# The weighted sum over V in a fused attention and gated feed-forward kernel: V made the stationary operand in 64x32 array tiles, two head groups at once, with the output turned by VectorE transposes and packed by DMA

## The chip, the cores and the metric

The kernel runs on one core of a Trainium2 chip. The metric is the device time of one execution in microseconds (us), median over several executions. Executions of one kernel agree to about 0.3%.

## The reference

A block of a transformer on a sequence of 2,048 tokens of width 576: a layer norm, then sliding-window attention (32 heads of width 18, window 256) and a gated feed-forward of width 4,608 on the same normalised input, multiplied together and added to the input.

```python
xn = layernorm(x)                                   # [2048, 576]
q, k, v = split(xn @ wqkv)                          # 32 heads, Dh = 18
scores = q @ k.T * 18**-0.5                         # masked: 0 <= i - j < 256
s = (softmax(scores) @ v) @ wo
h = sigmoid(xn @ w_gate) * (xn @ w_up)              # F = 4608
out = x + s * silu(h @ w_down)
```

## The kernel before

The tokens are handled in four chunks of 512. (Two memories are named below: SBUF holds the operands, PSUM the results of matmuls.) In each chunk the kernel projects q, k and v, runs attention for eight groups of four heads, applies `wo`, and runs the feed-forward network. A list scheduler inside the program fixes the order of every engine's instructions before the launch, from a small table of estimated durations. It places gate/up and down matmuls wherever attention leaves TensorE free.

Scores are computed with keys on the partitions, so that after the exponential a tile `expr` holds [64 keys x queries]. For the weighted sum over V (called PV below) the kernel before makes `expr` the stationary operand and streams V (18 columns and a column of ones for the softmax sum), so each matmul has 19 or 38 moving columns. (The stationary operand sits in the array; the columns of the moving one stream past it.) The array is used as two tiles of 64 rows by 128 columns. In all code cuts here `...` stands for what is left out, some arguments are put in words, and comments are added.

```python
def pair(eng, outs, lhs, rhs, start, stop, swap=0):
    for i in range(2):                               # two 64-row tiles of the array
        t = i ^ swap
        res = eng.matmul(outs[i], lhs(ROWS[t], i), rhs(ROWS[t], i), ..., tile_position=(64 * t, 0))

# build_attn(c, hg): one PV group per group of four heads
for qb in range(BPC):                                # 4 blocks of 128 queries
    for t in range(2):
        ...
        for n, ks in enumerate(kss):                 # key blocks that all 128 queries see
            res = pair(eng, [b[:, o:o + VH] for b in outs],
                       lambda r, i: self.expr[r, se, t, qb * P:(qb + 1) * P],     # stationary, 64x128
                       lambda r, i: vpart(r, sub_pos(c, ks) * VSZ + hh), ...)     # moving, 64x19
        ...                                          # and one pair with 2 x 19 columns for the two edge blocks
# VectorE: two sums of two parts each, a reciprocal, two multiplies, per group
sm = op("DVE", ..., tensor_reduce(out[ROWS[i]], src, X, ALU.add))     # i = 0, 1
rc = op("DVE", 250, reciprocal(out[:, :, DH], out[:, :, DH]))
on = op("DVE", ..., tensor_tensor(o_tok[...], src, rr, ALU.mult))     # par = 0, 1
...
# build_wo(c): o_tok is turned by DMA transposes before the wo projection
te = self.flip(self.oT[:, so, :, :], self.o_tok[:, i, :], ...)
```

The softmax here doesn't subtract the row's maximum and nothing guards it: scores larger than these inputs give would overflow.

## Time and profile before

| what | value |
|---|---|
| time, median | 576.02 us (575.97 to 577.16, 3 runs) |
| span of the profiled execution | 575.1 us |
| PV on TensorE, first start to the next work's first start, 32 groups | 30.8 us |

The page's first part has, for each engine, the busy time, its share of the span and the count of instructions (PE is TensorE's matmuls, PEld its weight loads, DVE VectorE, ACT ScalarE, POOL GpSimd):

```profile
PE 568.3 (99%) x9324; PEld 358.6 (62%) x9324; DVE 339.1 (59%) x825; ACT 268.3 (47%) x379; POOL 176.7 (31%) x286
```

The page's fourth part is the chain of waits that ended last, followed back from the last instruction, as shares of the span by engine:

```profile
PE 94%; DVE 2%; DMA 1%; issue 1%; ACT 1%; POOL 1%; DVEq 0%
```

Both say TensorE (PE). They have to be read together: a busy share alone does not say who waits for whom, and the records of matmuls overlap.

The groups of instructions by line and shape (out<-in, shapes, count, busy us, mean ns of one, idle time before):

```profile
L99 PE MATMUL ps<-xnT,wgs 64*128 64x512 bf16 x2256 | 281.2, 376 | 0.0
...
L762 DVE TENSOR_REDUCE pvs<-ps 64x304 f32<-64x608 f32 x64 | 50.4, 787 | 11.9 <-PE ps L99 10.2
...
L99 PE MATMUL ps<-v_aug,expr 64*128 64x19 bf16 x1920 | 34.9, 168 | 0.0
...
L774 DVE TENSOR_TENSOR o_tok<-pvs 128x144 bf16<-128x144 f32 x64 | 16.8, 303 | 0.3
...
L766 DVE RECIPROCAL pvs<-pvs 128x16 f32<-128x16 f32 x32 | 8.0, 249 | 0.0
```

The lines L99 are matmuls, all of one helper; the tiles tell them apart. A 19-column matmul lasts 168 ns in its record, a 512-column one 376 ns: what both have in common is a latency of about 160 ns, which overlaps from one matmul to the next. So mean durations of matmuls must not be added. The three VectorE lines are the path behind PV: two reductions of 787 ns for each group, one reciprocal, two multiplies. For TensorE, what counts is the distance between starts, and the timeline shows it (start, length, engine, line, shapes, count):

```profile
351.67 0.83 PE L99 MATMUL ps<-xnT,wgs 64*128 64x512 bf16 x6
352.32 1.19 PE L99 MATMUL ps<-v_aug,expr 64*128 64x19 bf16 x80
353.33 0.40 PE L99 MATMUL ps<-xnT,wgr 64*128 64x512 bf16 x2
```

Three pairs of 512-column matmuls start at 351.67 and PV starts 0.65 us later, which is 0.215 us for each pair. PV's 80 matmuls then take until 353.33, the start of the next work: 1.01 us, or 25 ns for each of the 40 row pairs. All sums of PV below are made of start times in this way.

### The profile page before, as it was taken

Reading aid. Unit: us, or ns where it says so; the run is one execution under the profiler, and the core shown is the slowest. Engines: PE = TensorE matmul, PEld = TensorE weight load, DVE = VectorE, ACT = ScalarE, POOL = GpSimd, SP = SyncE. Lnnn points to the kernel's source line nnn. Section 1 sums busy time; section 2 is a strip of 40 time slices with the busy share of each in tenths; the row PEclk is TensorE's granted clock in tenths of the full one; section 3 lists DMA queues with packets and bytes.
Section 4 is the critical chain, followed back from the end, with each engine's and each line's share of the span. In section 5 each row is a group of like instructions: output and inputs, shape, how many; then the busy total and the mean of one; then the engine's idle time right before and its main releaser. Section 6 shows DMA issues by size and latency. Waiting matters only on the chain.

```text
span 575.1 us, 21060 instructions
## 1 busy us (share of the span) xinstructions
PE 568.3 (99%) x9324; PEld 358.6 (62%) x9324; DVE 339.1 (59%) x825; ACT 268.3 (47%) x379; POOL 176.7 (31%) x286
## 2 busy tenths in 40 slices
PE   9999999999999999999999999999999999999997
PEld 5555454679976565555676986554457754444786
DVE  5468988947978856678754677765321133333123
ACT  2247568437637557657640677555221023223111
POOL 5466454445476331544316361330000000000000
PEclk9999999999999999999999999999999999999999
DMA  7968968591213363343562113443650014442010
GB/s 228 292 191 192 243 188 186 149 171 34 71 44 85 113 126 107 96 129 86 107 96 51 48 33 89 131 121 94 176 145 23 23 59 141 138 146 75 1 43 23
DMA packets 115658, 64.65 MB, mean 112 GB/s; under 512 B 26060, under 2 KB 114204, under 8 KB 115568
## 3 DMA queue, kind: packets, MB, share of 16 engines
q1 hardware_dynamic: 110448, 58.57, 39.3%
q0 software_dynamic: 5120, 4.74, 3.2%
q8 instruction: 73, 1.20, 0.9%
q14 instruction: 17, 0.14, 0.1%
HBM read 51.61 MB, written 2.36 MB: 94 GB/s over the span
## 4 chain that ended last, share of the span: by engine, by line
PE 94%; DVE 2%; DMA 1%; issue 1%; ACT 1%; POOL 1%; DVEq 0%
PE ps L99 94%; DMA qk<-qd 1%; DVE hT L875 1%; POOL qk L255 1%; ACT tring L872 1%; DVE qd L583 0%; DVE s_attn L978 0%; ACT expr L696 0%; DVE thf L983 0%; ACT xnT L522 0%; DVE kx L661 0%; DVE xf L988 0%; PE ps L545 0%; DVE hT L419 0%; DVE small L487 0%
## 5 line engine op out<-in xcount | busy, mean ns | idle before, releaser
L99 PE MATMUL ps<-xnT,wgs 64*128 64x512 bf16 (+2 forms) x2384 | 287.9, 369 | 0.1
L99 PEld LDWEIGHTS ps<-xnT,wgs 64*128 64x128 bf16 x2384 | 112.3, 94 | 114.3 <-PE ps L99 1.4
L696 ACT ACTIVATE expr<-ps 128x1024 bf16<-128x1024 f32 (+2 forms) x160 | 156.2, 983 | 58.2 <-PE ps L99 57.4
L99 PE MATMUL ps<-wd_sb,hT 64*128 64x288 bf16 (+2 forms) x2448 | 155.8, 275 | 0.0
L875 DVE SCALAR_TENSOR_TENSOR hT<-tring,ps 128x512 bf16<-128x512 bf16 x144 | 98.7, 686 | 87.5 <-ACT tring L872 85.5
L872 ACT ACTIVATE tring<-ps 128x512 bf16<-128x512 f32 x144 | 85.8, 596 | 115.3 <-PE ps L99 114.0
L99 PEld LDWEIGHTS ps<-wd_sb,hT 64*128 64x128 bf16 x2448 | 118.7, 94 | 23.5
L255 POOL DMA_DIRECT2D qk<-qd x160 | 82.4, 523 | 92.7 <-DVE qd L583 42.9
L661 POOL TENSOR_SCALAR kx<-kprev,small 128x256 bf16<-128x256 bf16 x64 | 64.6, 1018 | 83.9 <-PE ps L99 83.4
L709 DVE TENSOR_TENSOR expr<-expr,mask 128x256 bf16<-128x256 bf16 (+2 forms) x232 | 65.4, 304 | 40.1 <-ACT expr L696 38.2
L99 PE MATMUL ps<-qk,kx 64*128 64x320 bf16 (+4 forms) x736 | 60.4, 251 | 0.0
L762 DVE TENSOR_REDUCE pvs<-ps 64x304 f32<-64x608 f32 x64 | 50.4, 787 | 11.9 <-PE ps L99 10.2
L99 PE MATMUL ps<-xnT,wgr 64*128 64x512 bf16 (+2 forms) x298 | 55.8, 369 | 1.5 <-DVE hT L875 1.1
L99 PEld LDWEIGHTS ps<-qk,kx 64*128 64x128 bf16 x736 | 32.9, 94 | 24.0 <-ACT expr L696 0.9
L968 ACT ACTIVATE thf<-ps 128x576 bf16<-128x576 f32 (+3 forms) x22 | 11.4, 520 | 69.0 <-PE ps L99 68.5
L99 PEld LDWEIGHTS ps<-v_aug,expr 64*128 64x128 bf16 x2432 | 35.6, 93 | 5.6 <-DVE hT L875 0.5
L99 PE MATMUL ps<-v_aug,expr 64*128 64x19 bf16 (+1 forms) x2432 | 36.0, 170 | 0.0
L99 PE MATMUL ps<-xnT,wqk 64*128 64x512 bf16 x256 | 32.9, 376 | 0.0
L971 DVE SCALAR_TENSOR_TENSOR thf<-thf,ps 128x576 bf16<-128x576 bf16 x12 | 9.1, 755 | 39.7 <-ACT thf L968 39.7
L661 DVE TENSOR_SCALAR kx<-qk,small 128x512 bf16<-128x512 bf16 x64 | 22.4, 380 | 7.0 <-DMA qk<-qd 6.5
L583 DVE CAST qd<-ps 128x1024 bf16<-128x1024 f32 (+1 forms) x20 | 22.3, 1116 | 6.6 <-PE ps L99 6.2
L643 ACT ACTIVATE v_aug<-ps 64x288 bf16<-64x288 f32 x32 | 13.1, 409 | 24.9 <-PE ps L99 24.4
(62 smaller groups left out, 274.6 us busy)
## 6 DMA issues: line engine op xcount, KB each, us to landing
wgs<-in_B_w_gate_dram SPq DMA_DIRECT2D x72, 256.0 KB, 3.0
wgs<-in_B_w_up_dram SPq DMA_DIRECT2D x72, 256.0 KB, 3.5
wd_sb<-in_B_w_down_dram SPq DMA_DIRECT2D x9, 576.0 KB, 5.9
qk<-qd POOLq DMA_DIRECT2D x100, 36.0 KB, 2.7
xf<-in_A_x_dram SPq DMA_DIRECT2D x16, 144.0 KB, 2.5
out_dram<-xf SPq DMA_DIRECT2D x16, 144.0 KB, 1.8
xr<-in_A_x_dram SPq DMA_DIRECT2D x6, 288.0 KB, 3.6
wqk<-in_A_wqkv_dram SPq DMA_DIRECT2D x2, 576.0 KB, 6.9
```

Of the source, the lines that this page charges most:

```text
L99: res = eng.matmul(outs[i], lhs(ROWS[t], i), rhs(ROWS[t], i), start=start, stop=stop, tile_position=(64 * t, 0))
L255: o = self.op(eng, DMA_ISSUE_NS[eng], lambda e: e.dma_start(dst, src), name, deps, prio, nbytes=nbytes)
L583: return eng.tensor_copy(dst, self.both(h, n))
L643: return eng.activation(dst, src, ACTF.Copy)
L661: return e.tensor_scalar(self.kx[:, sx, pos:pos + n_ // SW, t, :], src.rearrange("p (s k) -> p s k", k=SW), self.half[:, t:t + 1], None, A ...
L696: return eng.activation(self.expr[:, se, :, lo * SW:NT], self.both(h, NT)[:, :, lo * SW:NT], ACTF.Exp, scale=SM_SCALE)
L709: return eng.tensor_tensor(e_, e_, m_, ALU.mult)
L762: return eng.tensor_reduce(out[ROWS[i]], src, mybir.AxisListType.X, ALU.add)
L872: th = op("ACT", act_ns(NT), lambda e: e.activation(self.tring[:, st, :], bank(h, 0), ACTF.Tanh, scale=0.5), f"th:{c}:{ft}", deps=[pg, dt_ ...
L875: mu = op("DVE", dve_ns(NT), lambda e: e.scalar_tensor_tensor(self.hT[:, ft, :], self.tring[:, st, :], 1.0, bank(h, 1), ALU.add, ALU.mult) ...
L968: return e.activation(v2(t)[:, a:b, :], y2()[:, a:b, :], ACTF.Tanh, scale=0.25)
L971: q1 = op("DVE", dve_ns(w), lambda e: e.scalar_tensor_tensor(v2(t), v2(t), 1.0, y2(), ALU.add, ALU.mult), f"fq1:{nm}", deps=[th, f2], prio=0)
```

## The change

V becomes the stationary operand: a 64x19 piece of V sits in one 64x32 tile of the array and up to 320 columns of `expr` stream past it. Eight such tiles (two row halves, four column positions) hold the four heads of each of two head groups, one head to a tile, so PV now runs once for two groups. Its output has the head dimension on partitions, 32 apart, with queries along the free dimension, summed over the keys in PSUM. To normalise by the softmax sum it is turned by a VectorE transpose of 32x32 blocks, divided, turned back, and 18-row pieces are packed by DMA into `oT`, where the DMA transposes (`flip`) used to put it. To make room in SBUF the constants change too.

```diff
-NWS = 4          # slots of gate/up weights
+NWS = 3
-NEX = 8          # slots of exp tiles
+NEX = 12
+OENG = ("SP", "POOL")
+TURN_NS = 215.0
-NQD = 2          # slots for the projected q and k
+NQD = 1
-SPACE_NS = 800.0 # least distance of two score groups, for the scheduler
+SPACE_NS = 1100.0
...
+        self.pend += [(hg, where, ready)]
+        if hg % 2:
+            self.build_pv(c, hg // 2)
...
+        kss = [ks for ks in (0, 5, -4, -3, -2, -1, 1, 2, 3, 4, 6, 7) if c or ks >= 0]
+        span = {ks: (max(ks, 0), min(ks + 5, SPC)) for ks in kss}     # in blocks of 64 queries
+            for n, ks in enumerate(kss):
+                cols = slice(q0 * SW, q1 * SW)
+                for g, (hg, where, _) in enumerate(pend):             # two head groups
+                    for t in range(2):
+                        p0 = 32 * (2 * g + t)
+                        for i in range(2):
+                            res = eng.matmul(outs[i][p0:p0 + VH, cols], self.v_aug[ROWS[i], o:o + VH],
+                                             self.expr[ROWS[i], se, t, cols], start=n == 0, ...,
+                                             tile_position=(64 * i, p0), skip_group_check=True)
...
+        for i in range(2):
+            t1 = op("DVE", dve_ns(NT), f_t1, ...)                     # ot1 <- transpose(PSUM), fp32
+            rc = op("DVE", 200, reciprocal of the sums, deps=[t1])
+            on = op("DVE", ..., multiply into o2, deps=[rc, ...])
+            t2 = op("DVE", dve_ns(NT), transpose(o2T <- o2), ...)
+            for n, (k, r0, j0, i0, ni) in enumerate(self.o_moves(pr, i)):
+                o = self.dma(dst, sr, ..., deps=[t2, self.wo_last], eng=OENG[i])
...
-            te = self.flip(self.oT[:, so, :, :], self.o_tok[:, i, :], ...)
```

More of the change, by code (lines that the diff above doesn't have):

```diff
@@ L33 @@
 VSZ = (H // 2) * VH
-NOT = 4
 NQS = 4
 NKX = 2
-NEX = 8
+NEX = 12
+OENG = ("SP", "POOL")
+TURN_NS = 215.0
 BINS = (((-4, 0, 1), (1, 1, 5), (6, 6, 2)),
@@ L288, in alloc_memory @@
         self.tring, _ = seq("tring", [P, 2, NT])
-        self.v_aug, _ = seq("v_aug", [P, NVS * VSZ + VH])
+        self.v_aug, _ = seq("v_aug", [P, NVS * VSZ])
         self.qk, _ = seq("qk", [P, NQS, 2, NT])
@@ L295, in alloc_memory @@
         assert size([P, BPC, D], bf16) <= size([P, NEX, 2, NT], bf16)
-        self.o_tok, _ = seq("o_tok", [P, BPC, XW])
-        self.oT, _ = seq("oT", [P, NOT, KB, P])
+        self.ot1, _ = seq("ot1", [P, 1, NT], f32)
+        self.o2, _ = seq("o2", [P, 1, NT])
+        self.o2T, _ = seq("o2T", [P, 2, NT])
+        self.oT, _ = seq("oT", [P, KB, NT])
         self.s_attn, _ = seq("s_attn", [P, BPC, D])
@@ L319, in alloc_memory @@
         self.rstd = sm[:, 3 + 15 * NST:3 + 16 * NST].rearrange("p (s c) -> p s c", c=1)
-        self.pvs, _ = seq("pvs", [P, 1, 4 * BPC * (DH + 1)], f32)
         if self.verbose:
@@ L336, in build_graph @@
         self.r_ex = Ring(NEX, "expr")
-        self.r_pvs = Ring(1, "pvs")
-        self.r_oT = Ring(NOT, "oT")
+        self.r_ot1 = Ring(1, "ot1")
+        self.r_o2 = Ring(1, "o2")
+        self.r_o2T = Ring(2, "o2T")
         self.r_w = Ring(NWS, "wgs")
@@ L350, in build_graph @@
         self.op_pv = {}
-        self.op_on = {}
         self.op_s = {}
         self.op_q2 = {}
-        self.otr_last = []
+        self.wo_last = []
+        self.pend = []
+        self.op_o = {}
         self.prev_f2_last = None
@@ L452, in build_attn_consts @@
         self.op_vones = o
-        self.op_vzero = o = op("POOL", 100, lambda e: e.memset(self.v_aug[:, NVS * VSZ:NVS * VSZ + VH], 0.0), "init:vzero", deps=[o], prio=9)
+        self.op_o2z = o = op("POOL", 400, lambda e: e.memset(self.o2[:, :, :], 0.0), "init:o2z", deps=[o], prio=9)
         self.op_qz = o = op("POOL", 4300, lambda e: e.memset(self.qk[:, :, :, :], 0.0), "init:qz", deps=[o], prio=9)
@@ L714, in build_attn, with build_pv @@
             self.r_kx.release(sx, v_)
+        self.pend += [(hg, where, ready)]
+        if hg % 2:
+            self.build_pv(c, hg // 2)
+        if (c, hg) == (0, 1):
+            pv = self.op_pv[(c, hg)]
+            self.op_wo_w = [self.load_nat(self.wo_sb[:, :, :], self.wo, "dma:wo", ("wo",), 8, [pv])]
+            self.op_wo_w += self.load_rem(self.wor[:, :], (self.wo[:, 0:288], self.wo[:, 288:D]), "dma:wor", ("wor",), 8, [pv])
+    def build_pv(self, c, pr):
+        op = self.op
+        pend, self.pend = self.pend, []
         hp = self.pool_s.hold()
@@ L718, in build_attn @@
         vdeps = [self.op_v[kb] for kb in range(max(0, k0 - 2), k0 + BPC)]
-        vz = NVS * VSZ
-        def vpart(r, o):
-            return self.v_aug[r, o:o + VH]
+        kss = [ks for ks in (0, 5, -4, -3, -2, -1, 1, 2, 3, 4, 6, 7) if c or ks >= 0]
+        span = {ks: (max(ks, 0), min(ks + 5, SPC)) for ks in kss}
         def f_pv(eng):
             res = None
-            outs = self.halves(hp, 512)
-            for qb in range(BPC):
-                for t in range(2):
-                    o = (t * BPC + qb) * SW
-                    hh = (2 * hg + t) * VH
-                    kss = [ks for ks in range(2 * qb - 3, 2 * qb + 1) if c or ks >= 0]
-                    for n, ks in enumerate(kss):
-                        se = where[(ks, 2 * qb)]
-                        assert where[(ks, 2 * qb + 1)] == se
-                        res = pair(eng, [b[:, o:o + VH] for b in outs],
-                                   lambda r, i: self.expr[r, se, t, qb * P:(qb + 1) * P],
-                                   lambda r, i: vpart(r, sub_pos(c, ks) * VSZ + hh), n == 0, n == len(kss) - 1)
-                    a_, b_ = 2 * qb - 4, 2 * qb + 1
-                    se = where[(a_, 2 * qb)]
-                    assert where[(b_, 2 * qb + 1)] == se
-                    oa = sub_pos(c, a_) * VSZ + hh if c or a_ >= 0 else vz
-                    ob = sub_pos(c, b_) * VSZ + hh
-                    def two(r, i):
-                        v_ = vpart(r, oa)
-                        return bass.AP(v_.tensor, v_.offset, [v_.ap[0], (ob - oa, 2), (1, VH)])
-                    res = pair(eng, [b[:, o + VH:o + 3 * VH].rearrange("p (k d) -> p k d", k=2) for b in outs],
-                               lambda r, i: self.expr[r, se, t, qb * P:(qb + 1) * P], two, True, True)
-            return res
@@ L750, in build_attn @@
-        pv = op("PE", 40 * 24.7, f_pv, f"pv:{c}:{hg}", deps=[[m for m, _ in ready], vdeps, self.op_vzero, self.otr_last if hg else None], prio=1, acq=hp)
-        self.op_pv[(c, hg)] = pv
-        for se in sorted({se for _, se in ready}):
-            self.r_ex.release(se, pv)
-        pt, dp = self.r_pvs.produce()
-        out = self.pvs[:, pt, :].rearrange("p (g d) -> p g d", d=VH)
-        sums = []
-        for i in range(2):
-            def f_sum(eng, i=i):
-                b = hp.units[0] * 1024
-                src = self.ps[ROWS[i], b:b + 1024].rearrange("p (g w) -> p g w", w=SW)[:, :, 0:3 * VH].rearrange(
-                    "p g (k d) -> p g d k", d=VH)[:, :, :, 0:i + 2:i + 1]
-                return eng.tensor_reduce(out[ROWS[i]], src, mybir.AxisListType.X, ALU.add)
-            sm = op("DVE", dve_ns(608), f_sum, f"ps:{c}:{hg}:{i}", deps=[pv, dp], prio=1)
-            hp.release(sm)
-            sums.append(sm)
@@ L766, in build_attn @@
-        rc = op("DVE", 250, lambda e: e.reciprocal(out[:, :, DH], out[:, :, DH]), f"rc:{c}:{hg}",
-                deps=[sums], prio=1)
-        ons = []
-        for par in range(2):
-            def f_on(eng, par=par):
-                src = out[:, 8 * par:8 * par + 8, 0:DH].rearrange("p (t q) d -> p q t d", t=2)
-                dst = self.o_tok[:, :, RD + hg * 72:RD + (hg + 1) * 72].rearrange("p q (t i d) -> p q t i d", t=2, i=2)[:, :, :, par, :]
-                rr = out[:, 8 * par:8 * par + 8, DH:VH].rearrange("p (t q) d -> p q t d", t=2).broadcast_to([P, BPC, 2, DH])
-                return eng.tensor_tensor(dst, src, rr, ALU.mult)
-            on = op("DVE", dve_ns(144), f_on, f"on:{c}:{hg}:{par}", deps=[rc, self.otr_last], prio=1)
-            self.r_pvs.release(pt, on)
-            ons.append(on)
@@ L778, in build_attn @@
-        self.op_on[(c, hg)] = ons
-        if (c, hg) == (0, 0):
-            self.op_wo_w = [self.load_nat(self.wo_sb[:, :, :], self.wo, "dma:wo", ("wo",), 8, [pv])]
-            self.op_wo_w += self.load_rem(self.wor[:, :], (self.wo[:, 0:288], self.wo[:, 288:D]), "dma:wor", ("wor",), 8, [pv])
+            outs = self.halves(hp, NT)
+            for n, ks in enumerate(kss):
+                q0, q1 = span[ks]
+                cols = slice(q0 * SW, q1 * SW)
+                for g, (hg, where, _) in enumerate(pend):
+                    se = where[(ks, q0)]
+                    assert all(where[(ks, q)] == se for q in range(q0, q1))
+                    for t in range(2):
+                        o = sub_pos(c, ks) * VSZ + (2 * hg + t) * VH
+                        p0 = 32 * (2 * g + t)
+                        for i in range(2):
+                            res = eng.matmul(outs[i][p0:p0 + VH, cols], self.v_aug[ROWS[i], o:o + VH],
+                                             self.expr[ROWS[i], se, t, cols], start=n == 0, stop=n == len(kss) - 1,
+                                             tile_position=(64 * i, p0), skip_group_check=True)
@@ new lines, in f_pv, with f_t1 @@
+            return res
+        est = TURN_NS + sum(mm_ns((b - a) * SW) for a, b in span.values())
+        pv = op("PE", est, f_pv, f"pv:{c}:{pr}", deps=[[m for _, _, rd in pend for m, _ in rd], vdeps], prio=1, acq=hp)
+        for hg, _, rd in pend:
+            self.op_pv[(c, hg)] = pv
+            for se in sorted({se for _, se in rd}):
+                self.r_ex.release(se, pv)
+        for i in range(2):
+            p1, d1 = self.r_ot1.produce()
+            p2, d2 = self.r_o2.produce()
+            p3, d3 = self.r_o2T.produce()
+            o1 = self.ot1[:, p1, :].rearrange("p (b d) -> p b d", d=32)
+            o2 = self.o2[:, p2, :].rearrange("p (b d) -> p b d", d=32)
+            def f_t1(e, i=i, p1=p1):
+                return e.transpose(self.ot1[:, p1, :], self.halves(hp, NT)[i])
+            t1 = op("DVE", dve_ns(NT), f_t1, f"ot:{c}:{pr}:{i}", deps=[pv, d1], prio=1)
+            hp.release(t1)
+            rc = op("DVE", 200, lambda e, o1=o1: e.reciprocal(o1[:, :, DH], o1[:, :, DH]), f"rc:{c}:{pr}:{i}", deps=[t1], prio=1)
+            on = op("DVE", dve_ns(NT // 32 * DH), lambda e, o1=o1, o2=o2: e.tensor_tensor(
+                o2[:, :, 0:DH], o1[:, :, 0:DH], o1[:, :, DH:VH].broadcast_to([P, NT // 32, DH]), ALU.mult),
+                f"on:{c}:{pr}:{i}", deps=[rc, d2, self.op_o2z], prio=1)
+            self.r_ot1.release(p1, on)
+            t2 = op("DVE", dve_ns(NT), lambda e, p2=p2, p3=p3: e.transpose(self.o2T[:, p3, :], self.o2[:, p2, :]),
+                    f"ot2:{c}:{pr}:{i}", deps=[on, d3], prio=1)
+            self.r_o2.release(p2, t2)
+            for n, (k, r0, j0, i0, ni) in enumerate(self.o_moves(pr, i)):
+                dst = self.oT[r0:r0 + ni, k, :]
+                sr = self.o2T[32 * j0 + i0:32 * j0 + i0 + ni, p3, :]
+                o = self.dma(dst, sr, ni * NT * 2, f"dma:o:{c}:{pr}:{i}:{n}", ("o", pr, i), deps=[t2, self.wo_last], prio=1, eng=OENG[i])
+                o.slack = 1000.0
+                self.r_o2T.release(p3, o)
+                self.op_o.setdefault(c, []).append(o)
@@ new lines, in build_pv, with o_moves @@
+        if pr == 0:
+            self.op_o[c].append(op("DVE", dve_ns(NT, 4.0), lambda e: e.tensor_copy(self.oT[ROWS[1], 0, :], self.oT[ROWS[0], 0, :]), f"odup:{c}",
+                                   deps=[self.op_o[c], self.wo_last], prio=1))
+    def o_moves(self, pr, a):
+        runs = []
+        for j in range(4):
+            r = DH * (8 * pr + 2 * j + a)
+            i = 0
+            while i < DH:
+                k = 0 if r + i < RD else 1 + (r + i - RD) // P
+                end = RD if k == 0 else RD + k * P
+                n = min(DH - i, end - r - i)
+                p0 = r + i if k == 0 else (r + i - RD) % P
+                runs.append((k, p0, j, i, n))
+                i += n
+        return runs
@@ L785, in build_wo @@
         last = []
-        dup = op("DVE", 280, lambda e: e.tensor_copy(self.o_tok[:, :, 0:RD], self.o_tok[:, :, RD:2 * RD]), f"odup:{c}",
-                 deps=[self.op_on[(c, 0)], self.otr_last], prio=1)
         for i in range(BPC):
             qb = c * BPC + i
-            so, do = self.r_oT.produce()
-            te = self.flip(self.oT[:, so, :, :], self.o_tok[:, i, :], f"flip:o:{qb}", ("fo", so),
-                           deps=[[self.op_on[(c, hg)] for hg in range(NHG)], dup, do])
-            last.append(te)
+            cols = slice(i * P, (i + 1) * P)
             h2 = self.pool_s.hold()
@@ L797, in build_wo @@
             war = [self.op_q2[qb - BPC]] if c else []
-            wo = self.row_proj("wo", qb, h2, lambda r, k, so=so: self.oT[r, so, k, :], self.wo_sb, self.wor,
-                               [te, self.op_wo_w, war])
-            self.r_oT.release(so, wo)
+            wo = self.row_proj("wo", qb, h2, lambda r, k, cols=cols: self.oT[r, k, cols], self.wo_sb, self.wor,
+                               [self.op_o[c], self.op_wo_w, war])
+            last.append(wo)
             def f_se(eng, ss=ss, h2=h2):
@@ L808, in build_wo @@
             self.op_s[qb] = se
-        self.otr_last = last
+        self.wo_last = last
     def build_ffn(self, c):
```

## The prediction

> **What bounds the kernel now.** TensorE. The page's busy table has PE at 568.3 of 575.1 us (99%), and the chain of waits that ended last is 94% PE. PE's own idle time (group view) is some 10 us, mostly at the start. Gate/up matmuls fill every hole in attention, so PE time saved comes off the span nearly one for one; time saved on DVE, ACT or POOL hardly does.
>
> **What the change removes on PE.** PV is 2,432 matmuls in 32 groups. Start times in the timeline give 1.01 us per group of 80 (0.81 us per group of 64 in the first quarter): one row pair every 25 ns, although 19 columns need only 8 ns. In all 30.8 us.
>
> **What it adds on PE.** 16 groups of 96 (64 in the first quarter) matmuls with V stationary. The longest tile streams 2,560 columns (1,920). From the trace, 512 columns take 215 ns: 1.07 us (0.80) if all eight tiles run at once, 16.0 us in all. If each row pair still needs 25 ns, the narrow key blocks are issue-bound (100 ns per block of eight) and a group is some 1.37 us (0.96). The Trainium skill ("TensorEngine Tiling (Array Packing)", Key Properties) says that tiles are independent but that changing the tiling mode drains TensorE; this trace has no second mode in its steady part. My estimate of a drain is the latency of a tiny matmul, 168 ns in the trace, on entry, on exit or on both: 0.2 to 0.4 us per group. So about 1.5 us (1.2) per group, some 23 us in all: 8 us saved, 2.5 to 11.5 possible.
>
> **Moved elsewhere.** DVE loses 64 reductions (787 ns), 32 reciprocals (249 ns) and 64 multiplies (303 ns), 78 us; it gains 64 transposes of 128x512 (about 0.68 us each, as other 512-column passes), 32 reciprocals and 32 multiplies, about 66 us. Off the chain. The queues lose 16 flips (1.28 us of SP) and gain about 146 small DMAs, half on SP, half on POOL at 523 ns each (some 38 us); POOL has 177 us busy and stays off the chain, but attention gets later. Weight buffers fall from 4 to 3: each covers about 3.9 us of matmuls and lands in 3.0 to 3.5 us, so two ahead suffice, except perhaps in the DMA-heavy first 60 us (85% DMA share). One qd buffer instead of two delays projections, which fillers cover. I allow 1 us for new stalls of PE.
>
> **Prediction.** 576.0 - 8 + 1 = about 569 us, range 564 to 575. Faster by over 2% (under 564.5): 0.15; within 2%: 0.80; slower: 0.05.
>
> **What would show it right or wrong.** In the timeline, a PV group of 96 matmuls from its first start to the next work's: about 1.5 us. 1.25 us would mean hardly any drain and no issue limit; over 2.0, that the tiles do not run at once. PE's idle time in the group view should grow by under 3 us, and not by waits for gate/up weights. DVE busy should fall to about 325 us, POOL rise to about 215 us.
>
> **What would make it wrong.** Four column tiles reading different moving data from the same partitions may share bandwidth: PV would then cost 2 to 4 us a group, and the kernel 10 to 40 us more. SP waiting in order behind output-packing DMAs may starve the three weight buffers. The list schedule is fixed beforehand; if a transpose takes twice what it assumes, PSUM slots come free late and PE waits. Smaller drains than estimated would bring it to 2%.

## More of the kernel before

The gate/up tiles, which fill TensorE, are freed by VectorE: for each tile of 128 hidden units ScalarE takes a tanh out of PSUM, then VectorE's `hm` multiply (written to `hT`) reads the rest, and only then may the next tile use that PSUM.

PE waited for other engines for less than 3 us, and half of it at the start. The view of waits, for PE (who waited, for whom, us in total, times, longest):

```profile
PE ps L99 <- DVE hT L419: 1.3, 1, 1.3
PE ps L99 <- DVE hT L875: 1.1, 5, 0.3
PE ps L99 <- DVE small L487: 0.2, 1, 0.2
```

## The result, and the profile after

The changed kernel takes 567.67 us (567.22 to 567.86, 4 runs), the kernel before on the same chip 576.59 us (575.97 to 577.17, 4 runs). The ratio is 0.9844, with a 95% interval of 0.9827 to 0.9861: faster by 1.6%, within 2%. (Ratios here are the mean time of one kernel's fast runs over that of the other's of the same rounds, so not quite the ratio of the medians.) The result is correct.

The same lines of the page. Busy time of each engine:

```profile
PE 558.6 (99%) x8300; PEld 332.3 (59%) x8300; DVE 330.8 (58%) x793; ACT 267.8 (47%) x379; POOL 212.2 (37%) x358
```

Share of the chain of waits:

```profile
PE 96%; DVE 2%; ACT 1%; issue 1%; DVEq 0%
```

PE is still busy for 99% and still makes up the chain. VectorE (DVE) has 8 us less, GpSimd (POOL) 36 us more, which are the packing DMAs that it issues, and neither stands in the chain for more than 2%. PE's waits for other engines:

```profile
PE ps L100 <- DVE hT L891: 1.5, 4, 0.4
PE ps L100 <- DVE hT L423: 1.3, 1, 1.3
```

The groups of the new path (L750 is the new PV matmul, L768 and L776 are the two transposes, L771 the reciprocal, L772 the multiply):

```profile
L100 PE MATMUL ps<-xnT,wgs 64*128 64x512 bf16 x2256 | 283.6, 377 | 0.4
...
L776 DVE STREAM_TRANSPOSE o2T<-o 128x512 bf16<-128x512 bf16 x32 | 22.6, 706 | 0.5
L768 DVE STREAM_TRANSPOSE ot<-ps 128x512 f32<-128x512 f32 x32 | 22.4, 700 | 15.8 <-PE ps L750 15.7
...
L750 PE MATMUL ps<-expr,v_aug 64*19 64x320 bf16 x512 | 14.7, 297 | 0.0
...
L772 DVE TENSOR_TENSOR o<-ot 128x288 bf16<-128x288 f32 x32 | 14.5, 454 | 0.5
...
L771 DVE RECIPROCAL ot<-ot 128x16 f32<-128x16 f32 x32 | 8.1, 252 | 0.6
```

The VectorE lines sum to 68 us. The 320-column matmul's record is 297 ns long, of which 133 ns are columns: the latency is the same as in the old layout.

The timeline around one PV group:

```profile
176.81 0.81 PE L100 MATMUL ps<-xnT,wgs 64*128 64x512 bf16 x6
177.55 1.34 PE L750 MATMUL ps<-expr,v_aug 64*19 64x320 bf16 x96
178.82 0.61 PE L100 MATMUL ps<-xnT,wgs 64*128 64x512 bf16 x4
```

Read it as the one of before. Three pairs of 512-column matmuls, at 0.215 us each, start at 176.81, so the seventh matmul could start at 177.46. PV starts at 177.55: 0.09 us later. Its 96 matmuls, for two head groups, take 1.27 us until the next work starts, against 2.02 us for two groups before. The start times of the single records give more detail. The last 64-column matmul of PV is followed by the next work 122 ns later, although its columns need 27 ns, so there is a gap of 95 ns on the way out as well as 93 ns on the way in, the same in all 16 groups within 2 ns. Between them the columns stream for 1.18 us, where each tile has 2,560 columns, 1.07 us.

The records of weight loads tell where the gap lies: in all 16 groups PV's first weight load starts only 1 to 2 ns before its matmul, and the first one after PV 4 to 5 ns before its own (in the kernel before, PV's first weight load was 31 to 215 ns ahead). So the gap lies in front of the weight load and is not its duration.

Neither gap is visible as idle time. The record of a 512-column matmul is 377 ns long although its columns take 215 ns, and so covers the gap behind it. The Trainium skill ("Perfetto Trace Analysis", Tensor Engine Instruction (MATMUL, LD_WEIGHTS)) says that the profiler estimates the end of a matmul rather than observing it; this case agrees: the two 512-column records in front of the gap at 177.46 us are 376 ns long, like the others, and PE reads 99% in both kernels.

Where the time went, from the start times of all matmuls:

| | before | after |
|---|---|---|
| PV, first start to the next work's first start (after: with the gap on the way out) | 30.8 us | 19.1 us |
| gaps on the way into PV | 0.2 us | 1.4 us |
| gaps elsewhere, over 40 ns, after the first 13 us | 4.1 us | 4.9 us |
| the same in the first 13 us | 2.9 us | 2.6 us |
| sum | 38.0 us | 28.0 us |
| span | 575.1 us | 565.9 us |

(A gap is the distance from one matmul's start to the next one's, less its columns at 2.4 to the ns and 3 ns. Both figures are fitted to the distances of pairs of one width in these traces: 216 ns for 512 columns, 122 for 288, 109 for 256, 43 for 96.) The sum falls by 10.0 us (9.9 before rounding) and the span by 9.2. Of the rest, 0.5 us is in gaps under 40 ns, which rise from 0.6 to 1.1 us; what remains was not followed further.

### The profile page after: what moved, and what is told of

Its sections match the earlier page's. It is cut to its first block, busy times and chain, and to the rows that moved or that the text cites. A ratio compares the mean times of both kernels' runs of the same rounds, so it can differ in the third digit from the quotient of the medians.

```text
span 565.9 us, 19089 instructions
## 1 busy us (share of the span) xinstructions
PE 558.6 (99%) x8300; PEld 332.3 (59%) x8300; DVE 330.8 (58%) x793; ACT 267.8 (47%) x379; POOL 212.2 (37%) x358
## 4 chain that ended last, share of the span: by engine, by line
PE 96%; DVE 2%; ACT 1%; issue 1%; DVEq 0%
PE ps L100 93%; PE ps L750 3%; DVE hT L891 1%; ACT tring L888 0%; ACT expr L700 0%; DVE ot L768 0%; DVE s_attn L994 0%; DVE expr L713 0%; DVE thf L999 0%; DVE kx L665 0%; ACT xnT L526 0%; DVE o2T L776 0%; DVE o L772 0%; DVE xf L1004 0%; PE ps L549 0%
## 5 line engine op out<-in xcount | busy, mean ns | idle before, releaser
L100 PEld LDWEIGHTS ps<-xnT,wgs 64*128 64x128 bf16 x2384 | 109.2, 94 | 117.0 <-PE ps L100 4.4
L100 PE MATMUL ps<-wd_sb,hT 64*128 64x288 bf16 (+2 forms) x2448 | 153.6, 276 | 0.0
L100 PEld LDWEIGHTS ps<-wd_sb,hT 64*128 64x128 bf16 x2448 | 112.8, 94 | 27.9
L665 POOL TENSOR_SCALAR kx<-kprev,small 128x256 bf16<-128x256 bf16 x64 | 63.2, 995 | 60.4 <-PE ps L100 59.9
L256 POOL DMA_DIRECT2D oT<-o2T x72 | 36.9, 519 | 30.1 <-DVE o2T L776 16.9
L768 DVE STREAM_TRANSPOSE ot<-ps 128x512 f32<-128x512 f32 x32 | 22.4, 700 | 15.8 <-PE ps L750 15.7
L669 POOL COPY kprev<-qk 128x256 bf16<-128x256 bf16 x32 | 13.6, 427 | 40.1 <-DVE kx L665 38.8
L100 PEld LDWEIGHTS ps<-xnT,wgr 64*128 64x128 bf16 x298 | 14.7, 94 | 16.7 <-DVE hT L891 3.9
```

The lines of the kernel that those rows point to most:

```text
L256: o = self.op(eng, DMA_ISSUE_NS[eng], lambda e: e.dma_start(dst, src), name, deps, prio, nbytes=nbytes)
L665: return e.tensor_scalar(self.kx[:, sx, pos:pos + n_ // SW, t, :], src.rearrange("p (s k) -> p s k", k=SW), self.half[:, t:t + 1], None, A ...
L669: self.op_kp[hg] = op("POOL", 420, lambda e: e.tensor_copy(self.kprev[:, hg, :], self.qk[:, qs, 1, NT // 2:NT]), f"kp:{c}:{hg}", deps=[kxo ...
L768: return e.transpose(self.ot1[:, p1, :], self.halves(hp, NT)[i])
```

## The experiments

Theory A: TensorE bounds both kernels, and the whole gain is the shorter PV on TensorE, less the gaps at the change of array mode, less about a microsecond of new stalls. Rival B: the gain comes from lighter VectorE work. Rival C: it comes from the constants, that is the wider spacing of scores and the deeper ring of exp tiles. Twelve kernels were run. Three batches each had their own runs of the kernel before (medians 576.1 to 576.5 us) and the last single run too (576.4 us), so times can be compared across them, though they were run on three chips, to some 0.5 us. "The changed kernel" is 567.7 us.

### One head group after the other

```diff
-            for n, ks in enumerate(kss):
-                ...
-                for g, (hg, where, _) in enumerate(pend):
+            for g, (hg, where, _) in enumerate(pend):
+                for n, ks in enumerate(kss):
```

> The changed kernel, but the two head groups of a pair go through the array one after the other, so that four tiles run at once instead of eight; work, mode changes, order of all other instructions stay. Theory A (TensorE-bound; the gain is the shorter PV on TensorE and nothing else): each PV group streams its columns twice, 1.1 us more (0.82 us in the first quarter), 16.5 us in all, so about 584 us (581 to 588), slower than the kernel before. Rival B (the gain comes from lighter VectorE work and fewer queue waits): about 568 to 572 us.

Measured: 578.24 us (ratio 1.004 to the kernel before, 1.0025 to 1.0055), 10.6 us more than the changed kernel. The timeline of one PV group:

```profile
153.42 2.10 PE L750 MATMUL ps<-expr,v_aug 64*19 64x320 bf16 x96
155.46 0.61 PE L100 MATMUL ps<-xnT,wqk 64*128 64x512 bf16 x4
```

The group takes 2.04 us instead of 1.28 (1.44 instead of 0.94 in the first quarter), so 16 of them cost 11.1 us more (30.2 against 19.1 us from the start times). The gaps outside PV, counted as in the table, did not grow (7.0 us, after 7.5). That is the whole loss, and with it the whole gain: as four tiles instead of eight, with the same VectorE work, the same DMAs and the same constants, the changed kernel is slower than the kernel before. Rival B and rival C fall as the main cause. The expected size, 16.5 us, was too large, because the two halves were taken to follow one another strictly. They don't. The start times, grouped by width, in the middle of this group (ns from the span's start; in program order the second half's 320, 192 and 64 come after the first half's 256, 128 and 64):

```
width  matmuls  first start  last start   half
 320      4       154194       154203     first
 320      4       154210       154220     second
 256      4       154330       154339     first
 192      4       154353       154362     second
  64      4       154435       154444     second
 128      4       154439       154448     first
 128      4       154463       154473     second
  64      4       154495       154504     first
```

The second half's wide matmuls start ahead of earlier ones of the first half, since their tiles are idle. Matmuls of different column tiles started out of program order. The halves are told apart here by their widths, which is how the program orders them; the records carry no tile number.

### Extra changes of the array mode, and their control

```diff
+                if n in (1, 3, 5, 7):
+                    for i in range(2):                     # zeros, one column, added to the sums
+                        eng.matmul(outs[i][:, 0:1], self.zt[ROWS[i], :], self.zt[ROWS[i], 0:1], start=False,
+                                   stop=False, tile_position=(64 * i, 0), skip_group_check=True)     # 64x128
```

The control has `outs[i][0:VH, 0:1]` and `self.zt[ROWS[i], 0:VH]` in place of the first two operands, which is a 64x32 tile as its neighbours are.

> The changed kernel with four extra one-column matmul pairs of zeros in each PV group, in the 64x128 mode, so four extra round trips between array modes per group, 64 in all. If the 93 ns gap read at the entry and the 95 ns at the exit of PV are the price of a mode change: 64 x 0.19 = 12 us more, about 580 us (577 to 583). Rival (those gaps are a late semaphore or the end of a dependency, not the mode): under 571 us.

> Control of the run with extra mode changes: the same four extra one-column pairs of zeros per PV group, but 19 columns of stationary in the 64x32 mode, so no mode change. Mode theory: at most 1 us more, 567.5 to 569 us. Rival (any extra small matmul that breaks into the stream costs that much): about 580 us.

Measured: 581.30 us with mode changes, 569.44 us without. The control cost 1.8 us, a little more than the 1 us expected: PV itself grew by 1.0 us, and the rest is stalls elsewhere. The difference of the two is 11.9 us for 64 round trips: 0.185 us each, close to the 93 and 95 ns read from the trace. PV's start times alone, which leave out stalls elsewhere, give 33.0 against 20.1 us, 0.20 us each. The timeline with mode changes (L747 is the inserted pair):

```profile
155.75 0.33 PE L756 MATMUL ps<-expr,v_aug 64*19 64x320 bf16 x8
156.01 0.18 PE L747 MATMUL ps<-zt 64*128 64x1 bf16 x2
156.12 0.30 PE L756 MATMUL ps<-expr,v_aug 64*19 64x192 bf16 x16
156.35 0.18 PE L747 MATMUL ps<-zt 64*128 64x1 bf16 x2
156.46 0.33 PE L756 MATMUL ps<-expr,v_aug 64*19 64x128 bf16 x16
```

And the control:

```profile
151.27 0.33 PE L756 MATMUL ps<-expr,v_aug 64*19 64x320 bf16 x8
151.41 0.17 PE L747 MATMUL ps<-zt 64*19 64x1 bf16 x2
151.42 0.33 PE L756 MATMUL ps<-expr,v_aug 64*19 64x192 bf16 x18
...
152.00 0.16 PE L747 MATMUL ps<-zt 64*19 64x1 bf16 x1
152.01 0.30 PE L756 MATMUL ps<-expr,v_aug 64*19 64x320 bf16 x1
152.01 0.16 PE L747 MATMUL ps<-zt 64*19 64x1 bf16 x1
```

The first eight 320-column matmuls are followed by the inserted pair 0.26 us after their start with the mode change and 0.14 us without. From the inserted pair to the next PV matmul it is 0.11 us against 0.01 us. So the gaps belong to the change of mode and not to a semaphore or to a small matmul as such. Over the 16 groups they cost the change 16 x 0.19 = 3.0 us.

The last three lines confirm the starts out of program order, here by source line: the program has both matmuls of the inserted pair before the 320-column one, which started ahead of one of them, at 152.007 and 152.010 us. So it is in 12 of the 16 groups.

### PV's transposes twice

```diff
+    def twice(self, e, dst, src):          # the second one waits for the first; program order unchanged
+        e.transpose(dst, src).then_inc(self.sem_x, 1)
+        e.wait_ge(self.sem_x, self.nx)
+        return e.transpose(dst, src)
```

> The changed kernel with every VectorE transpose of the PV path done twice (64 more of 0.70 us each, 45 us more VectorE work; same program order on all engines). Theory A: VectorE has slack, only PSUM is held 0.7 to 1.4 us longer per group: 568 to 571 us. Rival B (VectorE work sets the time, so its 10 us saved are the gain): well over 575 us.

Measured: 598.56 us, 31 us more. This is a clear miss for theory A as it was put, and it needed an explanation. The chain of waits:

```profile
PE 81%; DVE 15%; issue 3%; ACT 1%; POOL 0%; DVEq 0%
```

VectorE's share of the chain went from 2% to 15%, while it was busy for only 62% of the span. PE's waits:

```profile
PE ps L100 <- DVE hT L899: 11.2, 11, 2.6
PE ps L100 <- DVE ot L796: 9.5, 8, 2.2
```

A part of VectorE's timeline after a PV group (L794 and L796 are the doubled transposes):

```profile
160.79 0.72 DVE L794 STREAM_TRANSPOSE ot<-ps 128x512 f32<-128x512 f32 x1 [2.00 <-PE ps L750]
161.54 0.72 DVE L796 STREAM_TRANSPOSE ot<-ps 128x512 f32<-128x512 f32 x1
...
164.01 0.71 DVE L794 STREAM_TRANSPOSE o2T<-o 128x512 bf16<-128x512 bf16 x1
164.76 0.71 DVE L796 STREAM_TRANSPOSE o2T<-o 128x512 bf16<-128x512 bf16 x1
165.40 0.68 DVE L794 STREAM_TRANSPOSE ot<-ps 128x512 f32<-128x512 f32 x1
166.11 0.72 DVE L796 STREAM_TRANSPOSE ot<-ps 128x512 f32<-128x512 f32 x1
```

The chain of VectorE work behind each PV group stands in a fixed order in front of other work on VectorE: here six transposes with the projection's cast, the reciprocal and a multiply between them take 6 us. The gate/up multiplies (`hT`) and the casts that free PSUM for TensorE come behind it, and PE waits. VectorE had slack on average, but not at those places in the order.

### The same, with the scheduler told

```diff
-            t1 = op("DVE", dve_ns(NT), f_t1, ...)
+            t1 = op("DVE", 2 * dve_ns(NT), f_t1, ...)          # and so for the second transpose
```

> As the run with the PV transposes doubled (598.6 us, 31 us more than the changed kernel), but the list scheduler is told that they take twice as long, so it may place other work around them. If the 31 us came from a fixed VectorE order, in which the gate/up multiplies that free PSUM stand behind a longer PV burst: under 575 us. If VectorE capacity sets the time after all (rival B): 590 us or more.

Measured: 574.63 us. PE's longest waits for VectorE are now short:

```profile
PE ps L100 <- DVE hT L899: 3.6, 9, 0.6
PE ps L100 <- DVE ot L796: 1.5, 2, 1.2
```

The same doubled work costs 7 us when the order is made for it and 31 us when it is not. So 24 of the 31 us came from the fixed order and not from VectorE's capacity. The other 7 us are real: more VectorE work of this kind is not free here, only far cheaper than its own 39 us of busy time (369.4 against 330.8 us in the pages).

### Less VectorE work in the kernel before

```diff
-                return eng.tensor_reduce(out[ROWS[i]], src, mybir.AxisListType.X, ALU.add)
+                return eng.tensor_copy(out[ROWS[i]], src[:, :, :, 0])         # wrong result on purpose
```

> The kernel before, order unchanged, with its 64 reductions of 787 ns replaced by copies of the first of the two addends (about 0.44 us each; the result is wrong on purpose), so 22 us less VectorE work. Theory A (VectorE not on the chain in the kernel before; its lighter load explains none of the gain): at least 574.5 us. Rival B: 571 us or less.

Measured: 575.71 us, ratio 0.9987 (0.997 to 1.0004). The group in this run, for the 787 ns of before:

```profile
L762 DVE COPY pvs<-ps 64x304 f32<-64x304 f32 x64 | 30.1, 471 | 11.9 <-PE ps L99 10.4
```

VectorE has 64 x 0.316 = 20 us less to do and the kernel gains 0.8 us; the interval allows for 1.7 us at most. The change itself lightens VectorE by only 8 us. So rival B falls for the gain: taking VectorE work away brings next to nothing, although adding it in the wrong place costs much. (The order was not made anew for the lighter work here. That such an order does not carry the gain either is shown by the run with one head group after the other, which has the changed kernel's order and VectorE work and is slower than the kernel before.)

### Three key blocks of PV

```diff
-            for n, ks in enumerate(kss):
+            for n, ks in enumerate((0, 5, 4)):                       # wrong result on purpose
```

> The changed kernel with only 3 of the 12 (8) key blocks of PV (768 of 2,560 or 1,920 columns; the result is wrong on purpose), everything else in the same order. Theory A (TensorE time of PV comes off one for one): 12 x 0.75 + 4 x 0.48 = 10.9 us less, about 557 us (555.5 to 559). If another engine is now close behind: 562 us or more.

Measured: 556.98 us, 10.7 us less than the changed kernel, with 10.9 expected. The timeline of one group:

```profile
149.14 0.52 PE L750 MATMUL ps<-expr,v_aug 64*19 64x320 bf16 x24
149.59 1.04 PE L100 MATMUL ps<-xnT,wqk 64*128 64x512 bf16 x8
```

The group takes 0.45 us instead of 1.28 (and 0.94 in the first quarter), 11.9 us less in all (7.2 against 19.1). So PV's time on TensorE still comes off nearly one for one: in the changed kernel nothing else is close behind TensorE.

### The constants of the change in the kernel before

All four constants (`NWS` 3, `NEX` 12, `NQD` 1, `SPACE_NS` 1100), then the weight ring alone, then the spacing alone:

```diff
-NWS = 4
+NWS = 3
-NEX = 8
+NEX = 12
-NQD = 2
+NQD = 1
-SPACE_NS = 800.0
+SPACE_NS = 1100.0
```

> The kernel before with the constants of the change alone: 3 weight slots instead of 4, 12 exp slots instead of 8, 1 qd slot instead of 2, spacing of scores 1.1 us instead of 0.8. Theory A: they were paid to make room and bring nothing, 575.5 to 579 us. Rival C (the gain is the better spaced schedule and the deeper exp ring): under 572 us.

> The kernel before with 3 weight slots and nothing else changed. All constants of the change together cost it 5 us (581.5). If the weight ring is the cost: 579 to 582 us. Rival (the spacing of scores and the single qd slot are): 576 to 577.5 us.

> The kernel before with the wider spacing of scores (1.1 us) and nothing else changed. All constants of the change cost it 5.0 us, the weight ring alone 1.5 us. If the spacing, which saves the changed kernel 4.4 us, fits only the changed kernel's order: 578 to 581 us here. Rival (the wider spacing is good for both, and the rest of the 5 us is the single qd slot): 573 to 576 us.

Measured: 581.51 us with all four (ratio 1.0087), 578.02 us with the weight ring alone (1.0025), 576.72 us with the spacing alone (1.001, interval 0.9994 to 1.0027). Rival C falls: in the kernel before the constants bring nothing and cost 5 us together, more than theory A had expected (579 us at most). PE's longest wait in the run with all four was one of a kind that the kernel before does not have:

```profile
PE ps L99 <- DMA wgs<-in_B_w_gate_dram: 1.9, 1, 1.9
```

The weight ring alone accounts for 1.5 of the 5 us, less than its expected range, and its trace has one wait of the same kind and length:

```profile
PE ps L99 <- DMA wgs<-in_B_w_gate_dram: 1.5, 1, 1.5
```

The spacing accounts for none of it, which neither expectation for that run had. The remaining 3.5 us belong to the single `qd` slot, to the 12 exp slots, or to the four together. That was not taken apart.

### The constants of the change in the changed kernel

```diff
-NWS = 3                          # first run
-NEX = 12
+NWS = 4
+NEX = 10
-SPACE_NS = 1100.0                # second run
+SPACE_NS = 800.0
```

> The changed kernel with 4 weight slots and 10 exp slots instead of 3 and 12 (the same memory). If the smaller weight ring costs the changed kernel something (its trace shows no wait of TensorE for a weight load, but eight 0.23 us waits between two halves of one gate/up tile where nothing stood between them): up to 2 us faster, about 566 us. Rival: the exp ring is the one that matters, since a pair of head groups needs 10 slots and the next pair could not start: 569 to 573 us.

> The changed kernel with the old spacing of scores, 0.8 us. If the wider spacing is part of the gain (it keeps exps from bunching up in front of ScalarE): 569 us or more. Theory A (gain is PV alone; spacing shuffles stalls of a microsecond): 566.5 to 569 us.

Measured: 570.49 us with 4 weight slots and 10 exp slots, 572.09 us with the old spacing (five executions, 571.64 to 574.16). Both are worse than the changed kernel, by 2.8 and 4.4 us. In the first the rival's range was right: this memory is better spent on exp slots, of which a pair of head groups holds ten at once. (Both rings changed in that run, so what the fourth weight slot alone does was not shown.) In the second theory A missed: the spacing, neutral in the kernel before, is worth 4.4 us here. The gaps between matmuls tell that both lose by stalls of PE: summed as in the table above, gaps over 40 ns of any kind are 10.4 us in the changed kernel, 13.4 us in the first run and 17.1 us in the profiled (slowest) execution of the second. Why the wider spacing suits the changed kernel's order was not shown.

So the constants belong to the change: it would have brought 4 us less with the old spacing. No version that beats the changed kernel was found.

## Why the prediction was right

The prediction was 569 us with a range of 564 to 575; the measurement is 567.67 us.

- "PE time saved comes off the span nearly one for one" held. PV with its gaps fell from 31.0 to 20.5 us in the table, 10.5 us, and the span by 9.2. Taking more columns away (10.7 us for 11.9) and running half the tiles at a time (10.6 us for 11.1) moved the time in the same proportion.
- "Some 23 us in all: 8 us saved" was too careful, and the mis-sized term is, first, the cost of a PV group outside its streaming. A group with both gaps took 1.37 us, not 1.5. The drain was put at 0.2 to 0.4 us per group and is 0.19 (93 and 95 ns, confirmed at 0.185 by the runs with extra mode changes). The estimate took the latency of a tiny matmul, 168 ns, for each drain, and little more than half of that is what shows.
- "The narrow key blocks are issue-bound (100 ns per block of eight)" was wrong, and is the second mis-sized term. In the trace, the eight matmuls of a key block start 3 to 4 ns apart in the first four blocks of a group of 96 (in all blocks of a group of 64) and about 8 ns apart in the later ones, so that a block of eight takes 24 to 67 ns. (The weight loads are spaced in the same two ways; whether they set the pace was not tested.) The streaming of a group is 1.18 us, a tenth above the 1.07 of its columns, and not 1.37. Both errors went the same way, so the number did not come out right because errors cancelled: PV gave 10.5 us for the 8 predicted.
- The sign to look for, "about 1.5 us" from PV's start to the next work's, gave 1.27. It was a poor sign: it contains the gap on the way out and leaves out the one on the way in, which lies in front of PV's first matmul.
- "I allow 1 us for new stalls of PE" fits: gaps outside of PV rose by 0.5 us in the table, and another 0.8 us of the span lies in gaps under 40 ns or is unassigned.
- VectorE: 66 us for the new work was 67.6 (transposes of 700 and 706 ns); busy time came to 330.8 us, not 325. POOL came to 212, not 215.
- PE's idle time (span less busy; the prediction had put it at some 10 us) grew from 6.8 to 7.3 us, by less than the 3 us allowed, and no wait for gate/up weights appears. That the smaller weight ring does no harm was not shown beyond that: no run has four weight slots and all twelve exp slots, and in the kernel before the smaller ring costs 1.5 us.
- "DVE ... off the chain" is true of the run but too simple. What the doubled transposes showed is that the order of VectorE's instructions protects TensorE more than its light load does: of the 31 us, 24 were the order's and 7 the load's.

The warning that column tiles might share bandwidth for moving data did not come true: with eight tiles at once, the 2,560 columns of each took 1.18 us, for 1.07 at the rate of a single stream.

## What to carry to other kernels

When TensorE is the bound, compare matmul layouts by the distance between starts, and put a price on every change of array mode (0.19 us for a round trip here): running the tiles of two head groups at once is what made this layout pay; with the same two groups in one visit but one after the other, with no more mode changes, it was slower than the old layout. An engine with 40% idle time may still be critical in a fixed order; before adding work to it, look at which instructions stand behind that work and who waits for them, and let the scheduler know the new durations. Retune constants with the change: the same four cost the old kernel 5 us, and one of them was worth 4.4 us to the new one.

## What the Trainium skill lacked or had wrong

- "TensorEngine Tiling (Array Packing)", Key Properties, says that changing the tiling mode drains TensorE and gives no figure. The runs show 93 ns from 64x128 to 64x32 tiles and 95 ns back, 0.185 us for a round trip by the times of the pair of runs with and without 64 extra ones and 0.20 us by their start times. The runs agree with it that tiles run independently: eight 64x32 tiles streamed 2,560 columns each in 1.18 us.
- "TensorE: Matmul & The Clock Gate", Part 3, The mechanism, says that matmuls start and end strictly in program order. In the run with one head group after the other, four 320-column matmuls of the second half started at 154.210 us, ahead of four 256-column ones of the first half at 154.330 us that precede them in the program (told apart by their widths); in the control run a 320-column matmul started at 152.007 us, ahead of an inserted one at 152.010 us that precedes it (told apart by their lines).
- The same page, Measured speedup vs the span model, has about 4 ns for each further tile. The trace shows 3 to 4 ns in the first four blocks of a PV group of 96, but about 8 ns in the later ones, which the page does not give.
- "VectorE: DVE Perf Modes", The three transpose paths, has 311 ns for a 128x128 bf16 transpose. For 128x512 the trace shows 706 ns (bf16, SBUF) and 700 ns (fp32, from PSUM), which that page does not give.
- No page says that a mode change is hidden in the profile: the records of the matmuls in front of it cover the gap, and PE reads 99% busy.
